# Splitting the first drain into column halves, inside the PSUM pool of the stage before

## The chip, the cores and the metric

The kernel runs on one core of a Trainium2 chip. Times are device microseconds (us) of one execution; a kernel's time is the median of several. The profiled span is about 1.8 us shorter than the time of the same execution. TensorE is PE in the profile, VectorE is DVE, ScalarE is ACT, GpSimd is POOL; PEld is the weight load of TensorE.

A word on terms. To *drain* or *evict* is to copy a matmul result out of PSUM, the memory that TensorE writes. A *strand* is one of two dependent sequences that run beside each other on different engines. A *warming* matmul multiplies ones by ones into a tile that nobody reads, to keep TensorE from going idle. The *granted clock* is the share of full speed at which TensorE was let run. The *chain* is the work that ended last, followed back step by step to what released it. Of the tiles, hs holds rows of h, mv their mean and variance, sd and rs the square root and its reciprocal, u the normalised rows and UT their transpose.

## The reference

A layer in two parts over x of 2048 rows and 512 columns, in bf16: a spectral filter and a feed-forward block, each behind a layer norm and with a residual.

```
X = rfft2(layernorm(x)) * (w_r + i w_i)
h = x + irfft2(X)
r = relu(layernorm(h) @ w1 + b1)
out = h + (r * r) @ w2 + b2            # w1: 512 x 1792, w2: 1792 x 512
```

## The kernel before

The Fourier transforms are matmuls with tables. The inverse transform ends in T2, a tile with four slices (even and odd parts, real and imaginary). For each group of 128 rows, 16 in all, stages 5 and 6 turn T2 into rows of h, which are normalised, transposed and multiplied by w1. Groups 0 and 1 are the first chunk of the feed-forward part; until they are ready TensorE has nothing of that part to do. The code between the last spectral stage and the first feed-forward matmul is called the bridge here.

The last pieces of T2 are evicted by two engines:

```python
        if split:                                     # the last call of stage 4
            nc.scalar.copy(dst[:, 0:2], src[0][:, 0:2])          # T2[:, 0:2]
            nc.vector.tensor_copy(dst[:, 2:4], src[1][:, 2:4])   # T2[:, 2:4]
    ...
        if pr == 8:
            warm(mm_tile("idle")[:, 0:512], 3)
    ...
    ps.release()                                      # the PSUM pool of the middle part
    ...
    ps = ctx.enter_context(tc.tile_pool(name="ps2", bufs=3, space=bass.MemoryType.PSUM))
```

Then the bridge, in the new PSUM pool:

```python
    def s5_first(g):                                  # group 0: odd and even part apart
        two = [bank("p5o", "ph", 3), bank("p5", "pp", 3)]
        for e in range(2):
            for r in range(2):
                nc.tensor.matmul(two[e][:, 0:256], lhsT=T2[:, 2 * e + r, g]..., rhs=GI[:, 2 * r + e, :], ...)
        nc.scalar.copy(od[:], two[0][:, 0:256])
    def s5_whole(g):                                  # group 1: eight matmuls, one eviction
        pe = bank("p5", "pp", 3)
        ...
        nc.scalar.copy(R[:], pe[:])
    # s5b(0): R[:, 0:256] = even + od, R[:, 256:512] = even - od, on VectorE
    # s6(0):  py = xs/WSC + KI @ R;  hs = WSC * py on ScalarE, which also sums it
    # s6(1):  py = KI @ R;           s6a(1): hs = WSC * py + xs on VectorE
    s5_first(0)
    s5_whole(1)
    s5b(0)
    s6(0)
    s6(1)
    rest = [s5(2, True), s5(3, True)]
    idle = bank("idle", "ph", 3)
    s6a(1)
    s6b(0, True)                                      # sum of squares of group 0, ScalarE
    s6b(1)                                            # bn_stats, bn_aggr of group 1, VectorE
    nc.vector.tensor_scalar(mv2[:, 0, 0:1], mv2[:, 0, 0:1], 1.0 / D, None, ALU.mult)
    warm(idle[:], 9)
    for g in range(2):
        nc.scalar.activation(sd2[:, g:g + 1], mv2[:, g, 1:2], ACT.Sqrt, bias=eps[:], ...)
    for g in range(2):
        nc.vector.reciprocal(rs2[:, g:g + 1], sd2[:, g:g + 1])
        nc.vector.tensor_scalar(u2[:, g, :], hs[:, g, :], mv2[:, g, 0:1], rs2[:, g:g + 1], ALU.subtract, ALU.mult)
    rest[0]()
    for g, cp in ((0, nc.scalar.copy), (1, nc.vector.tensor_copy)):
        ...                                           # four transposes per group, one eviction to UT
```

## Time and profile before

| | before |
|---|---|
| time, median of 3 runs | 166.54 us |
| TensorE busy | 153.8 us, 93% of the span |
| bridge, from the start of VectorE's last T eviction to the first feed-forward matmul | 46.48 to 53.65, 7.17 us |
| feed-forward part, from there to the last output sum | 53.65 to 161.53, 107.88 us |

The feed-forward part is a wall of matmuls, and the change does not touch it. The bridge is a chain of short pieces, each of which waits for another engine. The lines that carry this stand in the prediction below, with how to read them.

### The profile page before, as it was taken

To read this page: it belongs to the slowest core of one execution; us is meant where nothing else is said; L and a number is where in the kernel's file an instruction comes from. 1 tells how busy PE (TensorE), PEld (TensorE's weight loads), DVE (VectorE), ACT (ScalarE), POOL (GpSimd) and SP (SyncE) were. 2 spreads that over 40 slices of the span, in tenths; PEclk is the share of its full clock that TensorE was granted. 3 is DMA by queue.
4 is the path that set the end of the run, shared out by engine and by line. 5 is a ranking of instruction groups with operands and counts; after the bars stand their busy time and mean duration, and the time that the engine had idled before them with its cause. 6 is when DMAs were issued, how large, how long until landed. Compare 5 with 4: busy or idle time off the path is not lost.

```text
span 164.8 us, 2760 instructions
## 1 busy us (share of the span) xinstructions
PE 153.8 (93%) x976; PEld 89.5 (54%) x976; DVE 126.3 (77%) x320; ACT 106.7 (65%) x201; POOL 37.9 (23%) x64
## 2 busy tenths in 40 slices
PE   3989999899998999898999999999999999999992
PEld 1356676687754874564445454444644444565471
DVE  6999899999947799589984579978479974468321
ACT  4899877999957880496932798460597654088100
POOL 7867850000100005022200223300023500044000
PEclk9999999999999999999999999999999999999999
DMA  4989399999000000100000100000200001000011
GB/s 149 359 279 91 80 187 189 389 360 149 2 0 0 4 0 2 66 4 0 0 32 32 36 0 2 0 32 32 68 2 0 0 32 36 32 32 0 0 64 32
DMA packets 12621, 11.42 MB, mean 69 GB/s; under 512 B 6976, under 2 KB 11072, under 8 KB 12608
## 3 DMA queue, kind: packets, MB, share of 16 engines
q1 hardware_dynamic: 12448, 10.33, 22.6%
q0 software_dynamic: 160, 0.92, 2.6%
q8 instruction: 7, 0.11, 0.3%
q14 instruction: 6, 0.05, 0.1%
HBM read 8.01 MB, written 2.10 MB: 61 GB/s over the span
## 4 chain that ended last, share of the span: by engine, by line
PE 68%; DVE 16%; ACT 5%; DMA 3%; POOL 2%; issue 2%; SPq 0%; ACTq 0%; DVEq 0%
PE po L827 28%; PE ph L794 25%; DMA xs<-in_A_x_dram 3%; PE p L346 2%; DVE mA L436 2%; PE po L815 2%; DVE mB L436 2%; ACT junk L209 2%; PE p L623 2%; PE p L679 2%; DVE Z L442 1%; POOL rs L224 1%; ACT rl L797 1%; DVE Z L443 1%; PE p L565 1%
## 5 line engine op out<-in xcount | busy, mean ns | idle before, releaser
L794 PE MATMUL ph<-UT,W 128*128 128x384 bf16 (+2 forms) x280 | 52.7, 336 | 1.2 <-DVE UT L881 0.6
L797 ACT ACTIVATE rl<-ph,b1f 128x384 bf16<-128x384 f32 (+2 forms) x70 | 41.7, 615 | 15.1 <-PE ph L794 13.6
L827 PE MATMUL po<-W,act 128*128 128x512 bf16 x210 | 47.3, 379 | 0.0
L801 POOL TENSOR_TENSOR hb<-hs,b2b 128x512 f32<-128x512 bf16 x16 | 18.9, 1184 | 89.2 <-DVE act L798 89.2
L794 PEld LDWEIGHTS <-W 128*128 128x128 bf16 x280 | 26.9, 98 | 21.1 <-issue 1.9
L798 DVE TENSOR_TENSOR act<-rl 128x384 bf16<-128x384 bf16 (+2 forms) x70 | 29.8, 458 | 10.1 <-ACT rl L797 10.0
L827 PEld LDWEIGHTS <-act 128*128 128x128 bf16 x210 | 20.3, 98 | 23.4
L831 DVE TENSOR_TENSOR ot<-po,hb 128x512 bf16<-128x512 f32 x15 | 10.3, 690 | 11.1 <-PE po L827 7.7
L257 PE MATMUL p<-ones 128*128 128x512 bf16 x23 | 8.2, 511 | 2.8 <-POOL ones L153 2.8
L627 DVE SCALAR_TENSOR_TENSOR hs<-p,xs 128x512 bf16<-128x512 f32 x15 | 10.0, 680 | 0.9 <-PE p L623 0.9
L683 ACT COPY UT<-p 128x768 bf16<-128x768 bf16 (+1 forms) x4 | 3.6, 906 | 10.9 <-PE p L679 10.9
L243 PE MATMUL p<-KFr,xs 128*128 128x256 bf16 x32 | 7.5, 277 | 1.2 <-DVE KFr L228 1.1
L571 ACT CAST V<-p 128x512 bf16<-128x512 f32 x14 | 8.4, 600 | 0.0
L217 DVE BATCH_NORM_STATS2 st<-xs 128x6 f32<-128x512 bf16 x12 | 7.9, 677 | 0.0
L257 PEld LDWEIGHTS <-ones 128*128 128x128 bf16 x35 | 3.9, 114 | 7.2 <-POOL ones L153 2.8
L245 PE MATMUL p<-KFr,xs 128*128 128x256 bf16 x32 | 7.3, 274 | 0.0
L638 ACT ACTIVATE junk<-hs 128x512 bf16<-128x512 bf16 x6 | 3.8, 627 | 5.5 <-DVE hs L627 5.5
L346 PE MATMUL p<-GF,Bt 128*128 128x256 bf16 x56 | 7.1, 273 | 0.0
L609 DVE TENSOR_TENSOR H<-V 128x254 bf16<-128x254 bf16 x14 | 6.9, 490 | 0.3 <-ACT V L571 0.2
L491 ACT CAST T<-p 128x1024 bf16<-128x1024 f32 x7 | 7.0, 1039 | 0.0
L623 PE MATMUL p<-R,KI 128*128 128x512 bf16 x15 | 5.7, 378 | 0.9 <-ACT rl L797 0.8
L655 ACT ACTIVATE sd<-mv,eps 128x2 f32<-128x2 f32 (+2 forms) x7 | 2.0, 295 | 6.7 <-DVE mv L642 6.6
(188 smaller groups left out, 239.2 us busy)
## 6 DMA issues: line engine op xcount, KB each, us to landing
W<-in_B_w_dram SPq DMA_DIRECT2D x2, 1792.0 KB, 10.6
out_dram<-ot SPq DMA_DIRECT2D x15, 128.0 KB, 1.8
xs<-in_A_x_dram SPq DMA_DIRECT2D x3, 512.0 KB, 6.2
WB<-in_A_w_r_dram SPq DMA_DIRECT2D x1, 578.2 KB, 6.2
WB<-in_A_w_i_dram SPq DMA_DIRECT2D x1, 578.2 KB, 7.5
xs<-in_A_x_dram SPq DMA_DIRECT2D x2, 256.0 KB, 3.6
b2b<-in_B_b_dram SPq DMA_DIRECT2D x1, 128.0 KB, 9.5
out_dram<-ot SPq DMA_DIRECT2D x2, 64.0 KB, 1.5
```

The lines of the kernel that those rows point to most:

```text
L217: nc.vector.bn_stats(st[:], xs[:, g, :])
L257: nc.tensor.matmul(o, lhsT=ones[:, 0:P], rhs=ones[:], start=True, stop=True)
L346: nc.tensor.matmul(puv[:, :, e, :], lhsT=Bt[:, 2 * t + 1 - e, 2 * pr + q, :], rhs=GFv[:, t, :, e, :], start=(t == 0), stop=(t == 1))
L571: nc.scalar.copy(V[:].rearrange("p e h c -> p (e h c)"), pe[:])
L623: nc.tensor.matmul(py[:], lhsT=KI[:], rhs=Rs.pop(g)[:], start=True, stop=True)
L627: nc.vector.scalar_tensor_tensor(hs[:, g, :], Ys.pop(g)[:], WSC, xs[:, g, :], ALU.mult, ALU.add)
L794: nc.tensor.matmul(ph[:, 0:n], lhsT=W1[:, d, bass.ts(f, P)], rhs=UT[:, d, 0:n], start=(d == 0), stop=(d == ND - 1))
L797: nc.scalar.activation(rl[:, 0:n], ph[:, 0:n], ACT.Relu, bias=b1f[:, f:f + 1], scale=1.0)
L798: sq = nc.vector.tensor_tensor(act[:, f, 0:n], rl[:, 0:n], rl[:, 0:n], ALU.mult)
L801: add = nc.gpsimd.tensor_tensor(hb[:, g, :], hs[:, g, :], b2b[:], ALU.add)
L827: nc.tensor.matmul(po[:], lhsT=act[:, f, bass.ts(i, P)], rhs=W2[:, f, :], start=(f == 0), stop=(f == NF - 1))
L831: nc.vector.tensor_tensor(ot[:], po[:], hb[:, g, :], ALU.add)
```

## The change

Its intent is to shorten that chain. Groups 0 and 1 are drained in the pool of the middle part, so that their first matmuls need not wait for the pool to close, which both evictions of T2 must precede. Group 1's eviction and the matmuls with KI come in halves of 256 columns. The small statistics instructions are put in a new order: group 0's go first. There are nine warming matmuls instead of twelve.

```diff
-            warm(mm_tile("idle")[:, 0:512], 3)
+            warm(mm_tile("idle")[:, 0:512], 2)
...
-    ps.release()                       # and the new pool, both moved behind the drain
...
+    halves = [mm_tile(f"p5{e}")[:, 0:256] for e in range(2)]
+    for e in range(2):
+        q5(halves[e], 0, 0, e, True, True)
...
+    nc.scalar.copy(od[:], halves[0])
+    for h, op in ((0, ALU.add), (1, ALU.subtract)):
+        nc.vector.tensor_tensor(R2[0][:, 256 * h:256 * h + 256], halves[1], od[:], op)
+        pe = mm_tile(f"p5w{h}")[:, 0:256]
+        for e in range(2):
+            q5(pe, 1, h, e, e == 0, e == 1)
+        nc.scalar.copy(R2[1][:, 256 * h:256 * h + 256], pe)
+    for g in range(2):
+        py = mm_tile("p6")[:, 0:512]
...
+        for h in range(2):
+            nc.tensor.matmul(py[:, 256 * h:256 * h + 256], lhsT=KI[:], rhs=R2[g][:, 256 * h:256 * h + 256], ...)
...
+    warm(mm_tile("idle")[:, 0:512], 3)
+    ps.release()
...
-    warm(idle[:], 9)
+    nc.vector.bn_stats(st1[:], hs[:, 1, :])
+    warm(idle[:], 4)
+    nc.scalar.activation(sd2[:, 0:1], mv2[:, 0, 1:2], ACT.Sqrt, bias=eps[:], scale=float(D) ** -3)
+    nc.vector.tensor_scalar(mv2[:, 0, 0:1], mv2[:, 0, 0:1], 1.0 / D, None, ALU.mult)
+    nc.vector.reciprocal(rs2[:, 0:1], sd2[:, 0:1])
+    nc.vector.bn_aggr(mv2[:, 1, :], st1[:])
+    nc.scalar.activation(sd2[:, 1:2], mv2[:, 1, 1:2], ACT.Sqrt, bias=eps[:])
```

`q5(o, g, h, e, first, last)` is a pair of matmuls of group g, half h, parity e into o.

More of the change, by code (lines that the diff above doesn't have):

```diff
@@ L538 @@
             nc.scalar.activation(junk1[:], eps[:], ACT.Sqrt, bias=eps[:])
-    ps.release()
     tab.release()
     fwd.release()
-    ps = ctx.enter_context(tc.tile_pool(name="ps2", bufs=3, space=bass.MemoryType.PSUM))
     ffn = ctx.enter_context(tc.tile_pool(name="ffn", bufs=1))
@@ L577, in s5, with s5b @@
         rest()
-    def s5_first(g):
-        two = [bank("p5o", "ph", 3), bank("p5", "pp", 3)]
-        for e in range(2):
-            for r in range(2):
-                nc.tensor.matmul(two[e][:, 0:256], lhsT=T2[:, 2 * e + r, g].rearrange("p q s -> p (q s)"),
-                                 rhs=GI[:, 2 * r + e, :], start=(r == 0), stop=(r == 1))
-        od = ffn.tile([P, 256], FP32, tag="od", bufs=4, name="od")
-        nc.scalar.copy(od[:], two[0][:, 0:256])
-        Rs[g] = two[1], od
-    def s5_whole(g):
-        pe = bank("p5", "pp", 3)
-        for h in range(2):
-            for k, lt in enumerate((1, 3, 0, 2)):
-                nc.tensor.matmul(pe[:, 256 * h:256 * h + 256], lhsT=T2[:, 2 * (lt % 2) + lt // 2, g].rearrange("p q s -> p (q s)"),
-                                 rhs=GIn[:, lt // 2, :] if h and k > 1 else GI[:, lt, :], start=(k == 0), stop=(k == 3))
-        Rs[g] = R = ffn.tile([P, 512], BF16, tag="R", bufs=3, name="R")
-        nc.scalar.copy(R[:], pe[:])
-    def s5b(g):
-        pe, od = Rs[g]
-        Rs[g] = R = ffn.tile([P, 512], BF16, tag="R", bufs=3, name="R")
-        if g == 0:
-            nc.vector.tensor_tensor(R[:, 0:256], pe[:, 0:256], od[:], ALU.add)
-            nc.vector.tensor_tensor(R[:, 256:512], pe[:, 0:256], od[:], ALU.subtract)
-            return
-        V, H = pe, od
+    def s5b(g):
+        V, H = Rs[g]
+        Rs[g] = R = ffn.tile([P, 512], BF16, tag="R", bufs=3, name="R")
         nc.vector.tensor_tensor(H[:, :, 1:128], V[:, :, 0, 1:128], V[:, :, 1, 1:128], ALU.add)
@@ L617, in s6 @@
         py = bank("p6", "pp", 3)
-        if g == 0:
-            nc.tensor.matmul(py[:], lhsT=identW[:], rhs=xs[:, 0, :], start=True, stop=False)
-            nc.tensor.matmul(py[:], lhsT=KI[:], rhs=Rs.pop(g)[:], start=False, stop=True)
-            nc.scalar.activation(hs[:, 0, :], py[:], ACT.Copy, scale=WSC, accum_out=mv2[:, 0, 0:1])
-            return
         nc.tensor.matmul(py[:], lhsT=KI[:], rhs=Rs.pop(g)[:], start=True, stop=True)
@@ L858, with q5 @@
     UTs[0] = ffn.tile([P, ND, 512], BF16, tag="UT", bufs=2, name="UT")
-    s5_first(0)
-    s5_whole(1)
-    s5b(0)
-    s6(0)
-    s6(1)
+    def q5(o, g, h, e, first, last):
+        for r in range(2):
+            nc.tensor.matmul(o, lhsT=T2[:, 2 * e + r, g].rearrange("p q s -> p (q s)"),
+                             rhs=GIn[:, r, :] if h and e == 0 else GI[:, 2 * r + e, :], start=(first and r == 0),
+                             stop=(last and r == 1))
+    halves = [mm_tile(f"p5{e}")[:, 0:256] for e in range(2)]
@@ new lines @@
+    for e in range(2):
+        q5(halves[e], 0, 0, e, True, True)
+    R2 = [ffn.tile([P, 512], BF16, tag="R", bufs=3, name="R") for g in range(2)]
+    od = ffn.tile([P, 256], FP32, tag="od", bufs=1, name="od")
+    nc.scalar.copy(od[:], halves[0])
[5 more added lines that the diff above has]
+        nc.scalar.copy(R2[1][:, 256 * h:256 * h + 256], pe)
@@ new lines @@
+    for g in range(2):
+        py = mm_tile("p6")[:, 0:512]
+        if g == 0:
+            nc.tensor.matmul(py, lhsT=identW[:], rhs=xs[:, 0, :], start=True, stop=False)
+        for h in range(2):
+            nc.tensor.matmul(py[:, 256 * h:256 * h + 256], lhsT=KI[:], rhs=R2[g][:, 256 * h:256 * h + 256],
+                             start=(g == 1), stop=(g == 1 or h == 1))
+        if g == 0:
+            nc.scalar.activation(hs[:, 0, :], py, ACT.Copy, scale=WSC, accum_out=mv2[:, 0, 0:1])
+        else:
+            nc.vector.scalar_tensor_tensor(hs[:, 1, :], py, WSC, xs[:, 1, :], ALU.mult, ALU.add)
@@ L864 @@
+    warm(mm_tile("idle")[:, 0:512], 3)
+    ps.release()
+    ps = ctx.enter_context(tc.tile_pool(name="ps2", bufs=3, space=bass.MemoryType.PSUM))
     rest = [s5(2, True), s5(3, True)]
     idle = bank("idle", "ph", 3)
-    s6a(1)
     s6b(0, True)
-    s6b(1)
+    st1 = ffn.tile([P, 6], FP32, tag="st", bufs=4, name="st2")
+    nc.vector.bn_stats(st1[:], hs[:, 1, :])
+    warm(idle[:], 4)
+    nc.scalar.activation(sd2[:, 0:1], mv2[:, 0, 1:2], ACT.Sqrt, bias=eps[:], scale=float(D) ** -3)
     nc.vector.tensor_scalar(mv2[:, 0, 0:1], mv2[:, 0, 0:1], 1.0 / D, None, ALU.mult)
-    warm(idle[:], 9)
+    nc.vector.reciprocal(rs2[:, 0:1], sd2[:, 0:1])
@@ L871 @@
+    nc.vector.bn_aggr(mv2[:, 1, :], st1[:])
+    nc.scalar.activation(sd2[:, 1:2], mv2[:, 1, 1:2], ACT.Sqrt, bias=eps[:])
     for g in range(2):
-        nc.scalar.activation(sd2[:, g:g + 1], mv2[:, g, 1:2], ACT.Sqrt, bias=eps[:], scale=1.0 if g else float(D) ** -3)
-    for g in range(2):
-        nc.vector.reciprocal(rs2[:, g:g + 1], sd2[:, g:g + 1])
+        if g == 1:
+            nc.vector.reciprocal(rs2[:, 1:2], sd2[:, 1:2])
         nc.vector.tensor_scalar(u2[:, g, :], hs[:, g, :], mv2[:, g, 0:1], rs2[:, g:g + 1], ALU.subtract, ALU.mult)
```

## The prediction

> **What bounds the kernel now.** I read the page first, then the chain that ended last in order of time, then the timeline of 46 to 54 us, where the changed code runs.
>
> The page, its engine line and its chain summary:
>
> ```profile
> PE 153.8 (93%) x976; PEld 89.5 (54%) x976; DVE 126.3 (77%) x320; ACT 106.7 (65%) x201; POOL 37.9 (23%) x64
> ...
> PE 68%; DVE 16%; ACT 5%; DMA 3%; POOL 2%; issue 2%; SPq 0%; ACTq 0%; DVEq 0%
> ```
>
> TensorE holds 68% of the chain, nearly all of it in the feed-forward part after 53.65 us. The change does not touch that part. It touches the bridge before it, where the chain hops between engines (chain in order of time: start, length, piece):
>
> ```profile
> 46.48 0.70 DVE T L489
> 47.18 0.14 issue
> 47.32 0.38 PE p5o L584 x2
> 47.70 0.22 PE p L584 x2
> 47.92 0.87 PE p L595 x8
> ...
> 49.47 0.38 PE p L623
> ...
> 49.88 0.70 DVE hs L627
> ...
> 51.33 0.18 DVE mv L642
> ...
> 53.65 1.91 PE ph L794 x16
> ```
>
> From the end of DVE's T eviction (47.18) to the first feed-forward matmul (53.65) lie 6.47 us, and all of it is latency: no engine is full, each piece waits for the one before. So a step shortened here counts in full, as long as it is on the longest of the parallel strands. Those show in the timeline (start, busy, engine, line, idle before it and what ended it):
>
> ```profile
> 46.26 0.59 ACT L488 CAST T<-p4a 128x512 bf16<-128x512 f32 x1 [0.18 <-PE p4a L464]
> 46.48 0.69 DVE L489 CAST T<-p4b 128x512 bf16<-128x512 f32 x1 [0.81 <-PE p4b L464]
> ...
> 47.78 0.37 ACT L587 COPY od<-p5o 128x256 f32<-128x256 f32 x1 [0.93 <-PE p5o L584]
> 48.24 0.42 DVE L604 TENSOR_TENSOR R<-p,od 128x256 bf16<-128x256 f32 x1 [1.07 <-ACT od L587]
> ...
> 48.83 0.59 ACT L598 CAST R<-p 128x512 bf16<-128x512 f32 x1 [0.68 <-PE p L595]
> ...
> 49.51 0.60 ACT L621 ACTIVATE hs<-p 128x512 bf16<-128x512 f32 x1
> ...
> 51.55 0.29 ACT L872 ACTIVATE sd<-mv,eps 128x1 f32<-128x1 f32 x1 [0.18 <-DVE mv L869]
> ```
>
> The reader is to see that ACT finished its half of T at 46.85 and DVE at 47.17, yet the first p5o matmul ran at 47.32: it waited for both, because the new PSUM pool opens only when the old one is closed, and three warming matmuls stood before it. Group 1's eviction on ACT is one 0.59 us piece that starts after all eight matmuls. Two strands then run side by side: group 0 on ACT (hs at 49.51, square at 50.23, sqrt at 51.08) and group 1 on DVE (hs at 49.88, statistics at 50.60, aggregate at 51.33, its sqrt on ACT at 51.55). Group 1 ends last (u at 52.17 to 52.58).
>
> **What the Trainium skill says.** "TensorE: Matmul & The Clock Gate", section "Back-to-back issue gap", gives N/2.4 + 2.5 ns per warm matmul, 109 ns at N = 256. The trace agrees: eight in 0.87 us. Its section "What's actually happening" has the clock halve after an idle window of some 3.4 us. The trace shows nothing of that in the bridge: the granted clock is 1.00 throughout, the longest idle of TensorE there is 0.61 us. "Advanced Engine Details and Errata", section "The Read-Write Bubble", says that a latency is exposed between the instructions of ScalarE and VectorE, so small tiles pay it each. The trace agrees: ACT takes 0.373 us for 256 columns (od) and 0.586 for 512 (R), so two halves cost 0.16 us more than a whole. "Perfetto Trace Analysis", section "Optimizing Scalar/DVE Operations", holds that where these engines are not saturated but cause bubbles elsewhere, breaking up instructions may complete work sooner. That is this change.
>
> **The change, part by part.** The compiled order of the changed kernel shows that the first pair of matmuls now waits for ACT's half of T alone, and the second pair for DVE's. One warming matmul fewer precedes them. All durations below are those of the trace before; the times are estimates from them.
>
> 1. First pair. Before, it ran 0.15 us after the last T eviction (47.17 to 47.32). Now 46.85 + 0.15 = 47.00. The two warming matmuls, at 0.216 us each from 46.28, are issued by 46.71 and don't bind. The pair takes 0.38, ACT's od starts 0.08 later as before: 47.46, ends 47.83. Gain 0.32.
> 2. DVE starts the sum 0.09 us after od (48.15 to 48.24 before): 47.92. The difference follows 0.34 us later, at 48.26, and ends 48.67 instead of 48.99.
> 3. The ten other matmuls run from 47.32, 0.109 us apart: the last at 48.30, ending 0.27 later at 48.57 (48.79 before). The sixth ends group 1's first half, at 48.14. ACT: first half 48.18 to 48.55, second 48.61 to 48.98. Before, the whole ended 49.42, gain 0.44. The extra 0.16 us of ACT lies in a gap.
> 4. TensorE: identity matmul at 48.41, first half of group 0 at 48.63, its second half 0.11 after DVE, as before (48.99 to 49.10): 48.78, ending 49.05. Group 1's second half at 49.02, ending 49.29. Total matmul time is as before, two of 256 for one of 512.
> 5. Group 0's strand: ACT hs at 49.08 instead of 49.51; its square and sqrt follow at the old distances, so sqrt0 runs 50.65 to 50.94. Gain 0.43.
> 6. Group 1's strand: DVE hs at 49.32 instead of 49.88; statistics 50.04 to 50.73 instead of 50.60 to 51.29. Gain 0.56.
> 7. Here the new order takes some back. The aggregate of group 1 now stands behind the scaling of group 0's mean and behind its reciprocal, which waits for sqrt0 at 50.94. So the reciprocal runs at 51.00, the aggregate at 51.08 to 51.26, although its input is there at 50.73: it idles 0.3 us. u of group 0 starts at 51.19 (51.66 before). sqrt1 runs 51.30 to 51.59 (51.55 before, gain 0.25 only), its reciprocal at 51.65 (51.98 before, where it stood behind u of group 0 for 0.14 after sqrt1), u of group 1 at 51.84 instead of 52.17. Gain 0.33.
> 8. From there nothing is changed: 1.48 us to the first feed-forward matmul, 53.32 instead of 53.65.
>
> The extra warming matmuls (three after the drain, four instead of nine later) lie in TensorE's waits: three from about 49.24 to 49.89, then the matmuls of groups 2 and 3 behind the release of the pool (DVE has read group 1's at 50.01, so about 50.15 to 50.6), then four to about 51.45, before the transposes at about 51.65. Gain: 0.33 us, taken as 0.35 because small queue latencies were rounded up. 166.54 - 0.35 = 166.19 us.
>
> **The rivals.**
> - *The halves wait for both T evictions after all, or the early pair gains nothing.* Then group 0 keeps od at 47.78, its strand gains only 0.11 (its last matmul being half as long), sqrt0 falls at about 50.97, and the aggregate behind it keeps sqrt1 where it was. Time 166.5. Against it: the compiled waits name one engine each.
> - *The aggregate behind sqrt0 costs more than I give it*, for instance if ACT's hs of group 0 must wait for the second R copy longer. Each 0.1 us more on ACT is 0.1 us of the time. 166.3 to 166.5. For it: group 0's strand now holds group 1's.
> - *The release of the pool.* TensorE cannot start groups 2 and 3 before DVE has read group 1's sum. If that came 0.3 us later than I think, the warming matmuls would run into the transposes of group 0 and, beyond a further 0.5 us, of group 1. The margin makes 166.2 stay; in the worst case 166.4.
> - *The clock.* Three warming matmuls fewer in all, 0.65 us less TensorE work. A drop to half speed for one window would add some 1.7 us (168). Against it: idle stretches stay well under one window.
> - *Later stages give the gain back.* After 67 us the chain passes through ACT and DVE up to 78.67, but these are fed by TensorE's own work after 53.65 and all loads have landed by 41 us, so the whole block shifts. Were it absorbed, 166.5.
>
> **Range and chances.** The steps can be off by some 0.05 us each, and two rivals end near 166.5; a gain larger than 0.56 has no source, except if step 7 costs nothing (0.45 then). So 166.19, eight times in ten within 165.95 to 166.45. Two per cent would be 3.3 us, half of the bridge: faster 0.01, within 0.98, slower 0.01.
>
> **What would show it.** Right: od near 47.46, the second R copy ending near 48.98, ACT's hs near 49.08 and DVE's near 49.32, idle on DVE between statistics and aggregate, sqrt1 near 51.30, first feed-forward matmul near 53.32, and everything after it shifted by the same amount. Wrong: od still at 47.78; a granted clock below 1.00; an idle TensorE before the transposes other than on u; or an equal first feed-forward matmul and a different end.

## The result

| | median | lowest to highest | runs |
|---|---|---|---|
| before | 166.53 us | 166.52 to 166.56 | 4 |
| changed | 166.02 us | 166.01 to 166.18 | 4 |

The ratio is 0.9971, with a 95% interval of 0.9954 to 0.9988. A ratio is the mean time of one kernel's runs over that of the other's in the same rounds, so not quite the ratio of the medians. The change is clear of the noise, but small: 0.51 us, 0.3%, well within the 2% that count as the same. The predicted time was 166.19 us, the range 165.95 to 166.45.

The page of the changed kernel, its engine line and its chain summary:

```profile
PE 152.9 (93%) x975; PEld 89.2 (54%) x975; DVE 126.6 (77%) x320; ACT 106.8 (65%) x202; POOL 37.3 (23%) x64
...
PE 69%; DVE 17%; ACT 4%; DMA 3%; POOL 2%; issue 2%; SPq 0%; ACTq 0%; DVEq 0%; POOLq 0%
```

The page as a whole hardly moved; a change of half a microsecond in a span of 164 has to be read from its own stage. Note that the profiled execution was the longest of the four, 166.18 us. Here is the load of x that stands in the chain (the third that is issued, rows of groups 4 to 7), start and length, of the kernel before and then of the changed one:

```profile
1.64 5.36 DMA xs<-in_A_x_dram
```

```profile
1.64 5.55 DMA xs<-in_A_x_dram
```

These rows landed 0.19 us later in that execution, and at the bridge VectorE's last T eviction began 0.13 us later, at 46.61 and not 46.48. The load comes long before any line that the change touches. So the changed kernel was run and profiled once more (166.01 us median, the profiled execution 166.04), and there the eviction began at 46.47, 0.01 from the kernel before. That profile can be laid beside the old one without a shift, and is used from here on. Its chain in order of time (start, length, piece):

```profile
46.89 0.72 PE p L829 x4
47.61 0.87 PE p5w L829 x8
...
48.70 0.23 PE p L850 x2
...
48.95 0.70 ACT hs L853 x2
...
50.52 0.30 ACT sd L865
...
50.85 0.16 DVE rs L867
51.01 0.08 DVE mv L868
...
51.65 0.42 DVE u L873
...
53.13 1.91 PE ph L761 x16
```

The bridge now takes 46.47 to 53.13, 6.66 us instead of 7.17: all of the 0.51 us. The feed-forward part takes 107.88 us as before (53.13 to 161.01), so nothing was given back. The path also changed engines: VectorE's T eviction is off the chain, and after the matmuls it runs through ScalarE and group 0 (hs, sd), where before it ran through VectorE and group 1.

The timeline of the same stretch (start, busy, engine, line, form, idle before it and what ended it):

```profile
46.47 0.69 DVE L489 CAST T<-p4b 128x512 bf16<-128x512 f32 x1 [0.81 <-PE p4b L464]
...
47.36 0.37 ACT L838 COPY od<-p 128x256 f32<-128x256 f32 x1 [0.53 <-PE p L829]
...
47.82 0.76 DVE L840 TENSOR_TENSOR R<-p,od 128x256 bf16<-128x256 f32 x2 [0.67 <-ACT od L838]
...
48.08 0.81 ACT L844 CAST R<-p5w 128x256 bf16<-128x256 f32 x2 [0.35 <-PE p5w L829]
...
51.12 0.29 ACT L869 ACTIVATE sd<-mv,eps 128x1 f32<-128x1 f32 x1 [0.31 <-DVE mv L868]
```

The first pair of matmuls runs at 46.89 while VectorE is still evicting (46.47 to 47.16). Group 1's two halves are done at 48.89 instead of 49.42. And the last line shows a longer wait: ScalarE is idle for 0.31 us before the second square root, until VectorE's aggregate, where before it was idle for 0.18 us.

### The profile page after: what moved, and what is told of

It is laid out like the page before. It is cut to its first block, busy times and chain, and to the rows that moved or that the text cites. A ratio compares the mean times of both kernels' runs of the same rounds, so it can differ in the third digit from the quotient of the medians.

```text
span 164.4 us, 2759 instructions
## 1 busy us (share of the span) xinstructions
PE 152.9 (93%) x975; PEld 89.2 (54%) x975; DVE 126.6 (77%) x320; ACT 106.8 (65%) x202; POOL 37.3 (23%) x64
## 4 chain that ended last, share of the span: by engine, by line
PE 69%; DVE 17%; ACT 4%; DMA 3%; POOL 2%; issue 2%; SPq 0%; ACTq 0%; DVEq 0%; POOLq 0%
PE po L794 28%; PE ph L761 25%; DMA xs<-in_A_x_dram 3%; DVE st L217 2%; PE p L346 2%; DVE mA L436 2%; PE po L782 2%; DVE mB L436 2%; PE p L646 2%; PE p L590 2%; DVE Z L442 1%; POOL rs L224 1%; ACT rl L764 1%; DVE Z L443 1%; PE p L563 1%
## 5 line engine op out<-in xcount | busy, mean ns | idle before, releaser
L594 DVE SCALAR_TENSOR_TENSOR hs<-p,xs 128x512 bf16<-128x512 f32 x14 | 9.4, 681 | 0.0
L376 ACT CAST U<-p 128x1024 bf16<-128x1024 f32 x6 | 6.2, 1058 | 0.0
```

The source lines that it names most:

```text
L594: nc.vector.scalar_tensor_tensor(hs[:, g, :], Ys.pop(g)[:], WSC, xs[:, g, :], ALU.mult, ALU.add)
```

## The experiments

There were twelve runs, of ten new kernels and two repeats, in three sets; each was timed beside the kernel before on the same chip. Times of the kernel before were 166.52 or 166.53 us, which is what lets a run be laid beside the changed kernel's 166.02 us from another chip. All results were correct. The expectations speak of the "first rows of x" that land late; the load in question is the third.

**1. The first pair waits for both halves of T2 again.** A dependency was added; nothing else differs from the changed kernel.

```diff
+            if g == 0 and e == 0 and r == 0:
+                after(mm, T_dve[0], "both halves of T")   # T_dve[0]: VectorE's eviction of T2[:, 2:4]
```

> The changed kernel, but its first pair of matmuls also waits for VectorE's half of T. Theory (the early pair is on the path to group 0's sum, and with it to everything after): the pair starts about 0.12 us after VectorE's T eviction, as in the kernel before, some 0.38 us later than in the changed kernel; od, the second half of R, hs of group 0 and its square root all move by about 0.38 to 0.40, and the time by the same: 166.02 + 0.38 = 166.40 us. Rival (the early pair only runs ahead of a TensorE that is busy with the other ten matmuls anyway, and ScalarE's eviction of group 1 sets when hs of group 0 starts): those ten end only some 0.2 us later, so at most 0.2 us: 166.2 us or less.

Measured: 166.40 us (166.39 to 166.65), as the theory has it; the rival's 166.2 is excluded. The early start is worth 0.38 us of the 0.51 when everything else is there.

**2. The same, with the wait split over two instructions.** A matmul of 32 columns takes the wait on ScalarE.

```diff
+            after(nc.tensor.matmul(idl[:, 0:32], lhsT=ones[:, 0:P], rhs=ones[:, 0:32], start=True, stop=True),
+                  T_act[0], "takes the wait on ACT")
```

> As the run before, but a tiny matmul takes the wait on ScalarE, so that the pair's weight load waits for VectorE's semaphore alone. Theory (part of the gain that I did not forecast is that a weight load which waits for two engines starts some 0.12 us after the later one, one that waits for a single engine some 0.05): the pair starts 0.05 us after VectorE's T eviction, and the time is 0.05 to 0.08 us below that of the run before. Rival (the difference of 0.07 us is the release of the PSUM pool, or chance): same time as the run before, within 0.03 us.

Measured: 166.37 us (166.31 to 166.52). Timeline of the T eviction, the weight loads and the matmuls in the first experiment (wait for two engines):

```profile
46.45 0.69 DVE L491 CAST T<-p4b 128x512 bf16<-128x512 f32 x1 [0.81 <-PE p4b L466]
47.26 1.22 PEld L831 LDWEIGHTS <-T 128*128 128x128 bf16 x12 [0.91 <-ACT T L490]
47.29 0.60 PE L831 MATMUL p<-GIa,T 128*128 128x256 bf16 x4 [0.44 <-DVE T L491]
```

and in this one (wait for one engine):

```profile
46.45 0.69 DVE L491 CAST T<-p4b 128x512 bf16<-128x512 f32 x1 [0.81 <-PE p4b L466]
...
47.20 1.21 PEld L834 LDWEIGHTS <-T 128*128 128x128 bf16 x12 [0.23 <-DVE T L491]
47.20 0.61 PE L834 MATMUL p<-GIa,T 128*128 128x256 bf16 x4
```

Both evictions end at 47.14. The matmul follows 0.15 us later where its weight load waits for two engines, as in the kernel before, and 0.06 later where it waits for one. The trace of the first experiment shows a separate EVENT_SEMAPHORE instruction of 51 ns ahead of the weight load, the kernel before has one too, and this run has none. The release of the PSUM pool is not the cause, since in both experiments the pool closes later. Nor is it that the small matmul left TensorE idle for less time: in experiment 8 (repeat) the first pair waits for ScalarE alone after 0.46 us of idle time and follows it by 0.06 us (46.81 to 46.87), while here in the first experiment it is 0.15 us after 0.44 us of idle time. The lead persists to the feed-forward part (53.49 and 53.42). In the medians it is 0.03, which the rival's "within 0.03 us" would allow, in the lowest times 0.08, so the traces carry the verdict and the size in time is only known as 0.03 to 0.08 us.

**3. Group 1 evicted whole.**

```diff
+    pw = mm_tile("p5w")[:, 0:512]          # one tile, both halves of the matmuls into it
-        nc.scalar.copy(R2[1][:, 256 * h:256 * h + 256], pe)
+    nc.scalar.copy(R2[1][:], pw)           # once, after all eight
```

> The changed kernel with group 1's R evicted by ScalarE in one piece of 512 columns, after all eight matmuls, instead of two halves. Theory (halving the eviction pays because ScalarE is free for hs of group 0 earlier): the whole runs from about 48.66 to 49.25 in the coordinates of the profile of the changed kernel, hs of group 0 starts 0.17 us later, and so does the end: 166.19 us. Rival (the half evictions gain nothing, because group 0's sum comes at 49.05 anyway and group 1's strand has slack behind the aggregate): 166.02 us. Second rival (group 1's strand is the longer): its hs starts 0.31 us later, 166.33 us.

Measured: 166.14 us (166.12 to 166.17), 0.12 more than the changed kernel. None of the three fits. The chain of this run (start, length, piece):

```profile
48.50 0.59 ACT R L845
...
49.14 0.39 PE p L851 x2
...
49.56 0.70 DVE hs L856
...
50.28 0.69 DVE st L864
50.98 0.05 DVE mv L867
```

Group 1's strand is now the longer one, as the second rival said, and its hs comes 0.31 us later (49.25 to 49.56). But some 0.2 of that falls into the time in which the aggregate would have waited for group 0 anyway, so the first feed-forward matmul comes only 0.10 later (53.23; 0.12 counted from each bridge's own start, 46.45 and 46.47). Group 0's hs starts at 48.99, 0.04 later and not 0.17: ScalarE begins it before the copy's reported end at 49.09.

**4. The KI matmuls whole.**

```diff
-        for h in range(2):
-            nc.tensor.matmul(py[:, 256 * h:256 * h + 256], lhsT=KI[:], rhs=R2[g][:, 256 * h:256 * h + 256], ...)
+        nc.tensor.matmul(py, lhsT=KI[:], rhs=R2[g][:], start=(g == 1), stop=True)
```

> The changed kernel with the KI matmuls of groups 0 and 1 in one piece of 512 columns, as before the change, all else new. Theory (the last of two halves ends 0.11 us earlier than a whole, and its weight load no longer waits for several semaphores together with VectorE): hs of group 0 starts 0.11 us later for the length, plus some 0.05 for the wait: 166.13 to 166.18 us. Rival (ScalarE, busy with group 1's second half until 49.03, sets the start of hs; TensorE's 49.05 is chance): no more than 0.1 us, 166.05 to 166.12.

Measured: 166.19 us (166.18 to 166.20), 0.01 above the theory's range and well above the rival's. TensorE's matmul on group 0's R begins at 48.66 and ScalarE's hs at 49.07; in the changed kernel the last half begins at 48.64 and hs at 48.95.

**5. Only the pool and the early pair**: whole eviction, whole KI matmuls and the old order of the small instructions, otherwise the changed kernel (the edits of 3 and 4, and the tail of the kernel before with four warming matmuls).

> The changed kernel with whole eviction, whole KI matmuls and the old order of the small instructions: what is left of the change is the early pair in the pool of the middle part, with the fewer warming matmuls. Theory: hs of group 0 waits for ScalarE's whole eviction, ending at about 49.25, some 0.37 us earlier than in the kernel before; hs of group 1 0.31 us earlier; with the old order group 1's u comes 0.32 us earlier: 166.21 us. So the early pair alone makes some two thirds of the gain of 0.51. Rival (the halves make most of it): 166.35 us or more.

Measured: 166.27 us (166.26 to 166.41), between the two, so neither claim holds: the early pair alone brings 0.26 us, half of the gain, and the halves with the new order the other half. With a whole eviction, ScalarE's copy at 48.52 to 49.11 binds. That is why the early pair brings 0.26 alone but costs 0.38 when undone: parts on one path are not worth a fixed sum each. The third warming matmul at the head is missing here too; by the spacing of the trace before (three of 0.216 us from 46.28) it would have held the pair back to 46.93, an estimate of 0.03 us.

**6. Only the new order of the small instructions, in the kernel before.**

```diff
-    s6b(1)                                  # bn_stats and bn_aggr together
+    nc.vector.bn_stats(st1[:], hs[:, 1, :])
+    ...                                     # sqrt, scaling and reciprocal of group 0, as in the change
+    nc.vector.bn_aggr(mv2[:, 1, :], st1[:])
```

> The kernel before with the new order of the small statistics instructions alone (aggregate behind group 0's reciprocal), nothing else of the change. Theory (the new order is no gain by itself: it makes group 1's aggregate wait for group 0's square root): u of group 1 comes 0.0 to 0.1 us later, 166.53 to 166.63 us. Rival (the new order frees u of group 0 earlier and is part of the gain): 166.3 to 166.45 us.

Measured: 166.57 us (166.55 to 166.59) against 166.53: no gain, as the theory said, and 0.04 us of loss.

**7. The aggregate first, in the changed kernel.**

```diff
     nc.vector.bn_stats(st1[:], hs[:, 1, :])
+    nc.vector.bn_aggr(mv2[:, 1, :], st1[:])
...
     nc.vector.reciprocal(rs2[:, 0:1], sd2[:, 0:1])
-    nc.vector.bn_aggr(mv2[:, 1, :], st1[:])
```

> The changed kernel with the aggregate of group 1 right behind its statistics, ahead of the scaling of group 0's mean and of its reciprocal. Theory (step 7 of the prediction: in the new order the aggregate waits for group 0's square root and takes back part of the gain): the aggregate runs at once after the statistics, ScalarE's second square root follows the first without idle time, the second reciprocal waits for u of group 0 alone, and u of group 1 comes 0.12 us earlier: 165.90 us. Rival (VectorE's order makes no difference, since u of group 0 and group 1 share VectorE anyway): 166.02 us.

Measured: 165.96 us (165.96 to 166.24), 0.06 less than the changed kernel's 166.02: half of what the theory had. Timeline of this run (its profiled execution started the bridge 0.26 us later than the changed kernel's, a late load again):

```profile
50.96 0.18 DVE L864 BATCH_NORM_AGGREGATE mv<-st 128x2 f32<-128x6 f32 x1
51.06 0.12 DVE L867 TENSOR_SCALAR mv<-mv 128x1 f32<-128x1 f32 x1
51.11 0.16 DVE L868 RECIPROCAL rs<-sd 128x1 f32<-128x1 f32 x1
51.18 0.29 ACT L869 ACTIVATE sd<-mv,eps 128x1 f32<-128x1 f32 x1
51.31 0.41 DVE L873 TENSOR_SCALAR u<-hs,mv,rs 128x512 bf16<-128x512 bf16 x1
```

Most of ScalarE's wait is gone: its second square root starts 0.11 us after the first is done (50.78 + 0.29 to 51.18). But u of group 1 still comes 0.52 us after u of group 0 (51.83), against 0.60 in the changed kernel: the second reciprocal now stands behind u of group 0 on VectorE, as the rival had it. I had taken 0.12 us for a wait of which 0.08 could be won.

**8. No warming matmuls in the bridge.** All nine were taken out.

> The changed kernel without any of the nine warming matmuls of the bridge. Theory (they do not lie on the path, and the idle stretches stay short of what lowers the clock): granted clock 1.00, the same time, 166.02 us within 0.05. Rival (the clock: without them TensorE is idle for some 2.5 of 4 us and the clock drops for a while at the start of the feed-forward part): matmuls of 256 columns some 0.21 instead of 0.11 us apart for a stretch, 167 to 168 us.

Measured: six executions, median 167.30 us: two at 166.02 and 166.08 us with a mean granted clock of 0.999 and 1.0, and four at 167.28 to 167.53 with 0.989. My theory fell; the rival was right, though not in every execution. The profile happened to catch a good one, so the kernel was run again:

> The changed kernel without its nine warming matmuls once more, to catch a slow execution in the profile. In four of six executions of the first try the mean granted clock was 0.989 and the time 167.3 to 167.5 us; the profiled one was a good one. Theory (the clock falls to half for one stretch of some 3.5 us, 0.011 of the span times two, begun by the idle time of TensorE in the bridge): if the profile falls on such an execution, the granted clock is about 0.5 in a stretch at the end of the bridge or the start of the feed-forward part, with matmuls of 256 columns 0.21 us apart, and 1.00 elsewhere. Rival (a small loss of clock spread over the whole run): no stretch stands out.

Measured: 167.62, 167.32 and 167.64 us, all with 0.988 to 0.99. Busy time by stretch in the profiled one (stretch and its length; busy us and count for PE, PEld, DVE, ACT and POOL; granted clock of TensorE; share and GB/s of the DMA engines):

```profile
52.00:53.00 1.00, 0.40 (x4) 0.23 (x4) 0.51 (x3) 0.52 (x1) 0.00 (x0) 1.00 0.00 0
53.00:54.00 1.00, 0.89 (x8) 0.79 (x9) 0.86 (x4) 0.20 (x1) 0.00 (x0) 0.90 0.00 0
54.00:55.00 1.00, 1.00 (x7) 0.69 (x6) 0.51 (x3) 1.00 (x4) 0.00 (x0) 0.50 0.06 16
...
57.00:58.00 1.00, 1.00 (x10) 0.86 (x9) 0.00 (x0) 0.58 (x3) 0.00 (x0) 0.89 0.00 0
58.00:60.00 2.00, 2.00 (x19) 1.70 (x18) 1.80 (x8) 1.82 (x6) 0.00 (x0) 1.00 0.00 0
```

The clock falls to one half shortly after the feed-forward part begins (53.11) and stays there for some 3.4 us: full losses from 54 to 57 and a tenth on either side, over one half. The first sixteen feed-forward matmuls take 2.94 us instead of 1.91. It costs 1.3 to 1.6 us, three times what the change gains, in seven of nine executions (one of the seven was profiled; the others have the same mean clock). So the warming matmuls are no idle luxury: with nine, none of the nine timed executions of the changed kernel shows it. How few would do was not tried. The longest idle stretch of TensorE here is 0.90 us. Against the changed kernel, the busy share of the bridge differs: 4.10 of 7.06 us, 58%, against 5.87 of 6.94, 85%, in its first profile. But the share cannot be all: the good execution that the first profile caught has the same 58% (4.11 of 7.06 us) and the same longest idle stretch, and its clock stayed at 1.00. What tips one execution and not another does not show in these traces, and that the share matters more than a single gap is only a reading. A rival was not tested either: the last eight matmuls of the bridge are transposes, and if these did not count as work, TensorE would have stood still from 50.60 to 53.11, 2.51 us.

**9 and 10. A version that beats both.** If halves help at the head of the bridge, they should at its tail, which the change left alone. On top of the aggregate first, group 1's transposed tile is evicted in two halves from two PSUM tiles:

```diff
-    for g, cp in ((0, nc.scalar.copy), (1, nc.vector.tensor_copy)):
+    for g, d0, n, cp in ((0, 0, 4, nc.scalar.copy), (1, 0, 2, nc.vector.tensor_copy), (1, 2, 2, nc.vector.tensor_copy)):
```

> The run with the aggregate first, and group 1's transposed tile evicted by VectorE in two halves from two PSUM tiles. Theory (the last 1.5 us before the feed-forward part, which the change left alone, are latency of whole pieces too): after two transposes the first half is copied, the first matmuls of the feed-forward part start some 0.25 us earlier and its third follows the second half without a wait: 165.74 us. Rival (the second half comes too late for the third matmul, or the squares' chain on ScalarE and VectorE takes the gain back): 165.9 us or more.

Measured: 165.71 us (165.68 to 165.72). Then u of group 1 in halves too:

```diff
+        for a in ((0, 256) if g else (0,)):
+            sl = slice(a, a + (256 if g else 512))
+            nc.vector.tensor_scalar(u2[:, g, sl], hs[:, g, sl], mv2[:, g, 0:1], rs2[:, g:g + 1], ALU.subtract, ALU.mult)
```

> As the run with the tail in halves, and u of group 1 made in two halves as well. Theory: the first two transposes start 0.14 us earlier, the second half of u ends only 0.06 later than the whole did: another 0.1 to 0.16 us, 165.6 us. Rival (the fixed cost of one more VectorE instruction eats it, as the second half then binds): the same as the run with the tail in halves, or slower.

Measured: 165.63 us (165.61 to 165.64), ratio to the kernel before 0.9946 (0.9933 to 0.996). The first theory held (165.74 expected); the second held in direction, with 0.08 us where it had 0.1 to 0.16. The first feed-forward matmul runs at 52.80 and 52.71, against 53.13, in bridges that begin within 0.03 us of each other. The second version beats both kernels, by 0.89 and 0.38 us.

**11. The changed kernel again**.

> The changed kernel unaltered, beside these runs on one chip, for a comparison of 0.1 us: 166.02 us in most executions, some 0.15 us more in those where the first rows of x land late. Rival for the gain as a whole (a matter of one chip or session): a time more than 0.1 us off that.

Measured: 166.01 us (166.00 to 166.04), ratio 0.997 (0.9956 to 0.9983). The gain of 0.51 us is not a matter of one session.

## Why the prediction was right

The prediction gave 166.19 us and the measurement 166.02: right in its direction and its mechanism, inside the range, and 0.17 us too cautious about a gain of 0.51. Its steps, against the profile of the repeated run:

| step | event | before | predicted | measured |
|---|---|---|---|---|
| 1 | first pair of matmuls | 47.32 | 47.00 | 46.89 |
| 1 | od on ScalarE | 47.78 | 47.46 | 47.36 |
| 2 | group 0's sum on VectorE | 48.24 | 47.92 | 47.82 |
| 3 | group 1's R complete | 49.42 | 48.98 | 48.89 |
| 5 | hs of group 0, ScalarE | 49.51 | 49.08 | 48.95 |
| 6 | hs of group 1, VectorE | 49.88 | 49.32 | 49.25 |
| 7 | aggregate of group 1 | 51.33 | 51.08 | 50.93 |
| 7 | second square root | 51.55 | 51.30 | 51.12 |
| 7 | u of group 1 | 52.17 | 51.84 | 51.65 |
| 8 | first feed-forward matmul | 53.65 | 53.32 | 53.13 |

**Step 1** was mis-sized: "Now 46.85 + 0.15 = 47.00". The 0.15 us was the lag behind the T eviction of a weight load that waited for two engines. The new one waits for one, and followed 0.05 us after ScalarE was done (46.84 to 46.89). This one term makes 0.11 of the 0.19 us by which the first feed-forward matmul came ahead of the forecast (the time was 0.17 off, as the prediction had rounded a gain of 0.33 up to 0.35). Experiment 2 shows the lag by itself, 0.15 against 0.06 us. "Perfetto Trace Analysis" of the Trainium skill, section "Identifying Dependency Chains", says that an instruction that waits on several engines may get extra semaphore instructions put ahead of it; it gives no cost. The trace agrees: the kernel before has one such instruction, of 51 ns, ahead of this weight load, and the changed kernel none. The prediction had seen in the compiled order that each wait names one engine, and did not ask what that alone would bring.

**Steps 2 and 3** held, shifted by step 1.

**Step 4** had the same flaw: its 0.11 us from VectorE's difference to the KI matmul was taken from a weight load that waited for VectorE and four DMA queues. In the changed kernel the second half's matmul came 0.06 us after VectorE (48.58 to 48.64). With this, hs of group 0 was 0.13 us ahead of the forecast where od had been 0.10 ahead. Experiment 4 measures halves and waits together, 0.17 us; it does not separate them.

**Steps 5 and 6** held, with the 1.57 us from hs to the first square root as before (48.95 to 50.52).

**Step 7** was right that the new order takes something back, and too high about how much. The aggregate does stand idle behind the reciprocal, for 0.27 us (50.66 to 50.93; the forecast was 50.73 to 51.08), and ScalarE waits 0.31 us for it; undoing it brings 0.06 us, not the 0.12 that step 7's 0.33 against the 0.45 "if step 7 costs nothing" implies, because VectorE itself is then in the way (experiment 7). Experiment 6 shows that the order alone gains nothing. The handovers in this step were each 0.01 to 0.03 us shorter than put down, about 0.06 in sum. With the 0.11 of step 1 and some 0.02 of step 4 this makes up the 0.19.

**Step 8** held: 1.48 us from u of group 1 to the first feed-forward matmul, and a feed-forward part of unchanged length.

Of the rivals, the wait for both evictions did not come, and experiment 1 shows what it would have cost: 166.40 where the prediction put 166.5. The release of the pool did hold up the matmuls of groups 2 and 3 until VectorE had read group 1's result (49.94 to 50.09), as estimated, and nothing on the path waited for them. The feed-forward part did not give the gain back. The clock rival was dismissed with the right outcome and a wrong reason: "idle stretches stay well under one window". Experiment 8 had such stretches, none above 0.90 us, and the clock fell all the same. What keeps the changed kernel from this is that nine warming matmuls were left in: none of its nine executions lost the clock, seven of nine without them did. The size that the prediction gave that rival, some 1.7 us, was near the measured 1.3 to 1.6.

## What to carry to other kernels

In a stretch where engines hand work to each other and none is full, give each consumer the smallest piece that it can start on, and let it wait for one producer only: a tile tracked in parts, a pool that need not close first, halves that two engines pass along. Read the value of each part from the path that is left when the others are in place, since parts on one path do not add up. And take the warming matmuls as one of the conditions under which the path was measured: before removing some, look at the granted clock of several executions, not of one.

## What the Trainium skill lacked or had wrong

- "TensorE: Matmul & The Clock Gate", sections "What's actually happening" and "Why this matters for your kernels", ties the fall of the clock to an idle window of some 3.4 us, or to idle gaps above some 3 us. Here the mean clock fell in seven of nine executions without the warming matmuls, and in the profiled one it halved with no idle gap above 0.90 us, after a stretch of 7.06 us with TensorE 58% busy. The page is not silent on short gaps: its section "A second HAM failure mode: psum-queue depth-cycling" tells of a kernel in which frequent short idles made the clock go up and down, but gives no share or length of gap at which this begins. The page's window does fit the length of the fall, some 3.4 us.
- "Perfetto Trace Analysis", section "Identifying Dependency Chains", mentions the extra instructions of a wait on several engines but no cost. The runs show one such instruction of 51 ns, and a matmul 0.15 us after the last producer with a wait on two engines, 0.05 to 0.06 with a wait on one.
- "Advanced Engine Details and Errata", section "The Read-Write Bubble", advises tiles of 512 or 1024 elements to keep the overhead small. On a latency path halves of 256 paid here in spite of their fixed cost: group 1's eviction took 0.81 us in halves and 0.59 whole, and undoing the halves cost 0.12 us. "Perfetto Trace Analysis", section "Optimizing Scalar/DVE Operations", has the rule that applies, and the runs agree with it.
- No page says how far the same load varies from execution to execution: the third load of x took 5.36 us in the profile before, 5.55 in the first of the changed kernel and 5.68 in that of experiment 7, and the bridge began 0.13 and 0.25 us later in the latter two.
